# A re-planned order for a recurrence followed by a two-layer MLP: GpSimd idle from block 9, TensorE's instruction pages in the plan, and wider products of zeros

## The chip, the cores and the metric

The kernel runs on one core of one Trainium2 chip. The metric is the device time of one launch in microseconds, as the median of three runs. The engines of the core are TensorE (PE in the profile; PEld is its loading of weights), VectorE (DVE), ScalarE (ACT), GpSimd (POOL) and SyncE (SP), which issues nearly all DMAs. All of them run their own instructions in order and wait for each other by semaphores.

## What is computed

A gated linear recurrence over 768 steps for 4 batches of 8 heads with head dimension 48, and then a two-layer MLP on the 3072 tokens of 384 features that it gives:

```python
def _attn_ref(q, k, v, alpha):
    B, H, S, D = q.shape                       # 4, 8, 768, 48
    state = np.zeros((B, H, D, D))
    for t in range(S):
        state = alpha[:, :, t, :, None] * state + einsum('bhd,bhe->bhde', k[:, :, t], v[:, :, t])
        y[:, :, t] = einsum('bhd,bhde->bhe', q[:, :, t], state)
    return y

def _moe_ref(x, w_in, w_out, s, b):            # w_in 384 x 2048, w_out 2048 x 384
    r = np.maximum(x @ w_in, 0.0)
    return (s * (r * r) + b) @ w_out
```

Inputs and outputs are float32. There is no expert routing in this case: every token goes through both products.

## The kernel before

The tokens are cut into 24 blocks of 128 steps, six for each batch. In each block the recurrence is done in chunked form: products on TensorE in place of 128 single steps, and a state of one 48 x 48 matrix for each head that is handed from block to block. The MLP works on groups of two blocks (256 tokens).

The kernel has no loop over blocks that sets the order. One string, ORDER, lists some 960 tokens, and the last lines of the kernel walk through it and call one small function for each token. The token's name says what is done, its number for which block or piece, and a prefix (D:, A:, P:) which engine does it where that isn't the default engine of the name:

```python
    for t in ORDER.split():
        eng, name, i = token(t)
        FN[name](ENG[eng or DEF[name]], i)
```

So ORDER fixes the order on every engine, and tables beside it (C_BANK, A_BANK, H_BANK and so on) fix in which of the 8 PSUM banks each result stands, and R_BANK which of 4 buffers takes each relu. ORDER and the tables come from a planner outside of the kernel.

The tokens that matter here, with the block or piece as their number:

- a, k, q, v (and pa, pk, pq, pv for pairs of blocks): loads on SyncE (L172, L188). i and o: loads of the four pieces of w_in and w_out in float32 (L258, L261); ci and co cast them to bfloat16.
- ln, cum, eb, ei, el: logarithm of alpha on ACT, its running sum on TensorE, and the exponentials of it on ACT (L368, L373).
- qb, kb: q and k times those exponentials, on DVE or GpSimd (L234, as `qk`). T with Tc (first blocks) or Td (a transposing DMA on SyncE, L426): their transposes.
- A: the products of keys and queries in a block (L481; L491 for the first six); mk: the mask on them, on DVE (L502, L508). KV, t, sn: the state (L439, L466, and L234 as `s_st`). vc: the cast of v.
- y (for blocks 0 to 5 the parts ya and ys): the block's result from mask and state (L530, L544, L561); ye: its copy to SBUF as `xd`.
- m0 to m95: the first MLP product, eight tokens for each group of two blocks, six matmuls of 256 columns each (L592). re: relu out of PSUM, on ACT (L599) or DVE (L601). sq: the square, on ACT (L609) or DVE (L234 as `gt`).
- w0 to w95: the second MLP product, four tokens for each block, four matmuls of 384 columns each (L626; L618 for the last block). oe: scale and bias on DVE. st: the store.
- z0 and so on: products of zeros into a bank that nothing reads, between the early tokens (L659). The table FILLS says how many, of what width.

Products A, y, ya, ys and the early KV use parts of the array (64 rows, or 32 columns); m, w, T, cum and the later KV use all of it.

In the order before, GpSimd has 69 tokens: masks and zeroed tiles at the start, casts of weights, and over the whole run 16 of the 24 kb, 13 of the 24 qb, 11 of the 16 sn and 8 of the 24 vc.

Of the kernel before, what the change touches and what calls it, by code (L numbers as in the profile page):

```python
# [40 lines left out]
R_BANK = [3, 0, 2, 1, 2, 1, 0, 3, 2, 0, 3, 1, 1, 1, 1, 2, 2, 0, 3, 1, 0, 0, 1, 2, 3, 1, 1, 3, 1,
2, 0, 2, 0, 1, 3, 2, 2, 0, 2, 1, 1, 2, 0, 3, 3, 2, 0, 1, 0, 1, 3, 3, 1, 2, 0, 3, 2, 3, 3, 1, 3, 2,
1, 0, 1, 2, 2, 1, 3, 0, 0, 3, 2, 0, 3, 1, 1, 0, 1, 1, 2, 0, 2, 0, 1, 0, 2, 2, 0, 3, 1, 2, 3, 3, 1,
1]
FILLS = [(0, 32, 128), (1, 12, 128), (1, 4, 128), (1, 15, 128), (7, 12, 128), (7, 6, 128)]


ORDER = """
zz0 Us0 P:zqk0 P:zla0 pre0 pa0 Ui0 zt1 sml0 pk0 pa1 ln0 P:zla1 zs1 ln1 zqk2 zvp1 z0 cum0 eb0 ei0
pq0 cum1 pv0 ln2 el1 ln3 pq1 ei1 pk1 mp0 D:zt0 zqk1 zs0 id0 P:kb0 pa2 qb0 kb1 zvp5 D:zvp0 z1 cum2  # L50
el0 eb1 cum3 P:qb1 z2 T0 pv1 ei2 D:zvp2 Tc0 D:vc1 eb2 A:vc0 eb3 i0 z3 A0 P:qb3 i2 mk0 zvp4 el3 ei3
qb2 T1 KV1 pq2 pk2 KV0 P:kb3 zvp3 A:Tc1 el2 z4 A1 ya0 P:kb2 vc2 t0 mk1 t1 z5 T3 ys1 ya1 ln4 ln5 T2
cum5 i3 Tc3 A:vc3 ye1 KV3 KV2 ye0 Tc2 sn1 A3 cum4 eb5 A2 t2 el5 ei5 mk3 ci0 P:ci1 zs2 pv2 i1 ys2
el4 eb4 ei4 sn2 m0 m1 mk2 ys3 t3 P:ci5 re1 ya3 ya2 D:ci4 re0 sq0 qb5 ye3 ye2 m5 qb4 m4 m8 m9 P:ci7
o0 re5 re4 a6 A:sq4 A:sq5 kb5 sq1 re8 T5 kb4 m13 re13 T4 Tc5 ci6 A:sq13 m12 A5 D:re9 Tc4 D:of0 mk5
m7 sn3 m6 A:sq8 vc5 m15 s0 D:vc4 D:re12 A:sq9 o3 A4 re6 re7 ci2 KV5 KV4 m14 mk4 ci3 A:sq12 o1 o2
re15 m2 ya5 a8 a7 a9 k7 k6 A:sq15 ya4 ys4 t4 D:sn4 ys5 q6 D:co1 D:re14 P:co0 D:re2 D:ye4 v6 m10 m3
w0 w8 sm0 sq7 ln6 q7 v7 k8 sq6 A:sq14 re3 ye5 re10 U0 m21 m16 A:sq10 m11 re21 A:sq21 co7 sq2 sq3
ca0 se0 D:re16 P:co6 cum6 D:co3 el6 re11 A:sq11 ei6 ca3 sq16 m23 m18 w12 m17 m19 re18 ln8 D:re23
D:co2 re19 eb6 re17 ln7 ca1 D:co5 w4 D:co4 cb0 w9 m20 ca2 cb1 kb6 sq17 A:sq18 w13 A:sq19 cc0 qb6  # L60
cd0 D:re20 a11 a10 m22 cum8 w10 w1 cum7 w5 w11 w2 ei8 el8 eb7 ln9 el7 re22 qb7 w6 w14 bm0 w3 eb8
w7 ei7 A:sq22 be0 oe0 sq23 D:vc6 A:sq20 A:vc7 Td6 P:kb7 w20 w16 KV6 w15 w21 cum9 oe2 Td7 q8 t6
ln10 ei9 ln11 oe1 oe3 eb9 w22 A6 A7 w17 w18 w23 mk6 cum10 mk7 y6 y7 q9 KV7 oe5 D:ye7 k9 v9 v8 q10
k10 w19 eb10 ei10 ye6 el10 cum11 m31 el9 t7 oe4 P:qb8 m26 P:qb9 D:re31 kb8 A:vc8 ei11 m25 m24
D:re25 D:re24 m27 A:sq25 m29 eb11 A:sq24 P:kb9 D:re26 P:qb10 k11 Td9 D:re27 D:vc9 P:kb10 A:sq31
KV8 m30 w24 q11 Td8 w28 re30 KV9 A:sq26 a12 sq30 D:re29 sn7 t8 D:sn8 A:sq27 m28 w25 re28 A:sq28
A:sq29 A9 Td10 v10 A8 w29 t9 w26 ln12 mk9 v11 a13 w27 w30 mk8 cum12 y8 y9 A10 P:kb11 w31 P:qb11
ye8 oe6 sn9 D:vc10 el12 ye9 ln13 mk10 vc11 eb12 m37 KV10 Td11 m34 oe7 m36 t10 q13 k13 cum13 k12
a15 D:re34 A11 re36 re37 mk11 m35 ei12 el13 sq36 m39 eb13 m32 sn10 re39 ei13 a14 q12 q14 y11 v13
qb13 sq39 sq37 kb12 ye11 y10 P:kb13 D:re35 ln15 ye10 D:re32 A:sq35 m38 m33 m46 cum15 D:re33 A:sq32  # L70
m44 A:sq33 a17 D:re46 ln14 D:re38 sq38 m45 m42 w36 m41 cum14 Td13 A:sq46 sq34 el15 D:re42 D:re44
ln17 m40 A:sq44 P:qb12 Td12 k14 v12 w37 re45 el14 w38 w39 ei14 eb15 ei15 D:re40 A13 D:vc13 sq45
oe9 A12 A:sq40 mk12 v14 w32 mk13 m43 w33 re41 sq41 a18 a16 w34 A:vc12 eb14 re43 P:kb14 KV12 A:sq43
v15 m47 q15 sq42 t12 w35 A:vc14 ln16 y13 y12 qb14 ye12 w44 D:ye13 re47 cum17 v19 k15 cum16 oe8 k16
eb16 A:sq47 ei17 KV13 P:qb15 m53 v16 Td14 t13 w40 m48 kb15 D:re48 eb17 ln18 el16 re53 ei16 KV14
m55 w41 m52 D:re55 m50 Td15 A:sq55 re52 m54 P:kb16 vc15 w45 KV15 m51 D:sn13 A:sq48 re54 q17 D:re50
t14 D:vc19 A14 mk14 sn14 A:sq50 A15 mk15 t15 w42 w46 A:sq52 q18 A:sq54 w47 m49 y14 re51 y15 oe11
k19 k17 P:qb17 vc16 D:re49 D:sn15 KV16 w43 q16 ye14 ye15 m59 a19 A:sq49 ln19 A:sq51 sq53 qb16 k18
a20 a21 q20 P:kb17 cum18 m57 oe10 w52 m61 Td16 re57 D:re59 Td17 m56 w53 m58 q19 v17 A:sq57 ei18
sq59 D:re61 v18 cum19 ei19 el19 el18 eb18 w54 t16 m63 re58 A:sq61 w55 m62 D:re63 D:re56 sn16 eb19  # L80
P:kb18 sq58 P:kb19 q21 a22 A16 A17 mk17 oe13 ln20 w48 w49 cum20 k20 k23 vc17 w50 m60 w51 D:re62
ei20 el20 eb20 A:sq56 mk16 re60 P:qb19 y17 y16 w56 ln21 A:vc18 a23 ye17 ln22 qb18 KV18 cum21 ye16
ei21 P:kb20 t18 KV19 w57 cum22 A:sq63 Td18 eb21 ei22 k21 m67 ln23 eb22 oe12 sq60 P:qb20 Td19 t19
sq62 m71 w60 el21 P:qb21 D:re71 D:re67 m68 m69 el22 m66 w61 A:sq71 kb21 k22 v20 D:re68 re66 w62
P:kb22 A:sq67 A18 A19 A:sq66 D:re69 cum23 w58 w63 Td20 mk19 m64 Td21 q22 sn19 y19 mk18 y18 D:ye18
eb23 ye19 w59 m65 ei23 A:vc20 v22 oe15 oe14 sq69 m72 re65 A21 A20 m70 A:sq65 P:qb22 re64 re72 mk21
mk20 vc22 v21 A:sq64 m76 re70 vc21 m79 KV20 st2 q23 st0 P:kb23 A:sq68 A:sq70 st11 Td22 st8 st3
re79 w64 t20 qb23 sq79 w65 KV21 D:sn20 t21 w66 w67 w68 m77 re76 oe16 re77 A:sq76 w69 sq72 Td23 m74
# [22 lines left out]
def kernel(  # L111
# [15 lines left out]
    B, H, S, D = q.shape  # L127
# [201 lines left out]
    def o_cum(e, u):  # L329
        la = la_sb[u % NLA]  # L330
        ct_ps = BANK[C_BANK[u]]
        cum = ct_ps[:, 0:384].rearrange("a (r h d) -> a r h d", r=2, h=NP)
# [34 lines left out]
    def o_eb(e, u):  # L367
        e.activation(  # L368
            out=b_sb[u % NB].rearrange("a h d -> a (h d)"), in_=BANK[C_BANK[u]][:, 0:384], func=AF.Exp
        )  # L370

    def o_ei(e, u):
        e.activation(  # L373
            out=binv_sb[u % NB].rearrange("a h d -> a (h d)"), in_=BANK[C_BANK[u]][:, 0:384], func=AF.Exp,
            scale=-1.0,
        )

    def o_el(e, u):
        if u < NPB:
            n, g = u - u % 2, u % 2  # L380
            e.activation(
                out=blast_sb[:, n % NBL : n % NBL + 2, 2 * g : 2 * g + 2],
                in_=BANK[C_BANK[u]][:, 384:388].rearrange("a (p c) -> a c p", c=2), func=AF.Exp,
            )
        else:
            e.activation(out=blast_sb[:, u % NBL], in_=BANK[C_BANK[u]][:, 384:388], func=AF.Exp)

# [22 lines left out]
    def tview(u):  # L410
        return BANK[T_BANK[u]].bitcast(BF16)

# [18 lines left out]
    def kv_view(n):  # L431
        return BANK[KV_BANK[n]][:, 0:384].rearrange("a (p e) -> a p e", p=NP)

# [220 lines left out]
        e.dma_start(out=out[n * C : (n + 1) * C, :], in_=out_sb[n % NOS])  # L654

    def o_z(e, x):
        bank, m, w = FILLS[x]
        for _ in range(m):
            nc.tensor.matmul(  # L659
                out=BANK[bank][:, 0:w], lhsT=zeros[:, 0:128], rhs=zeros[:, 0:w], start=True, stop=True  # L660
            )


    def tri64(t, strict):
# [106 lines left out]
```

## Time and profile before

| what | before |
| --- | --- |
| median of 3 runs | 178.77 us (178.53 to 179.05) |
| the profiled execution | 179.38 us, of which the span from the first to the last instruction is 177.7 us |
| granted TensorE clock | 1.0 over the span |
| busy: TensorE, DVE, ACT, GpSimd | 169.5, 134.0, 111.3, 54.6 us |
| first MLP product, L592, 576 matmuls | 72.0 us |
| second MLP product, L626, 368 matmuls | 68.1 us |
| GpSimd, qk from k, L234, 16 instructions | 17.0 us, 1066 ns each |
| GpSimd, qk from q, L234, 13 instructions | 13.4 us, 1031 ns each |
| products of zeros, L659, 81 matmuls | 7.2 us |

Busy times of matmuls overlap their neighbours at both ends, so a mean of 273 ns for a 256-column matmul isn't the distance between two of them. A "wait" is idle time of an engine ahead of an instruction, put down to the instruction or the DMA that ended it; "issue" is idle time for which the profile shows no wait. The slices of the page cut the span into 40 parts of 4.44 us; a window such as 66:83 is in us from the start of the span.

### The profile page before, as it was taken

To read this page: it belongs to the slowest core of one execution; us is meant where nothing else is said; L and a number is where in the kernel's file an instruction comes from. 1 tells how busy PE (TensorE), PEld (TensorE's weight loads), DVE (VectorE), ACT (ScalarE), POOL (GpSimd) and SP (SyncE) were. 2 spreads that over 40 slices of the span, in tenths; PEclk is the share of its full clock that TensorE was granted. 3 is DMA by queue.
4 is the path that set the end of the run, shared out by engine and by line. 5 is a ranking of instruction groups with operands and counts; after the bars stand their busy time and mean duration, and the time that the engine had idled before them with its cause. 6 is when DMAs were issued, how large, how long until landed. Compare 5 with 4: busy or idle time off the path is not lost.

```text
span 177.7 us, 5545 instructions
## 1 busy us (share of the span) xinstructions
PE 169.5 (95%) x2289; PEld 127.7 (72%) x2289; DVE 134.0 (75%) x239; ACT 111.3 (63%) x242; POOL 54.6 (31%) x83
## 2 busy tenths in 40 slices
PE   7898799899999999999999999999999999999992
PEld 7787597677656786687767868767767688877672
DVE  2298889999977999999887789496978779634421
ACT  3867689798662467367686857559649544956000
POOL 7686512400023715214022352634235302000000
PEclk9999999999999999999999999999999999999999
DMA  5999999999799969999989999999979993000352
GB/s 146 325 318 289 271 329 360 313 280 199 141 224 191 200 144 198 146 203 174 192 171 226 128 209 184 197 210 186 207 127 266 185 344 139 4 0 0 141 208 98
DMA packets 113708, 34.96 MB, mean 197 GB/s; under 512 B 106900, under 2 KB 112148, under 8 KB 113684
## 3 DMA queue, kind: packets, MB, share of 16 engines
q1 hardware_dynamic: 113684, 34.61, 87.8%
q8 instruction: 18, 0.29, 0.7%
q14 instruction: 6, 0.05, 0.1%
HBM read 25.17 MB, written 4.72 MB: 168 GB/s over the span
## 4 chain that ended last, share of the span: by engine, by line
PE 71%; DVE 7%; SPq 7%; ACT 6%; DMA 4%; issue 3%; POOL 1%; DVEq 0%; ACTq 0%
PE bank_ps L626 31%; PE bank_ps L592 28%; SPq L188 5%; DMA wst<-in_moe_w_in_dram 4%; PE bank_ps L481 3%; ACT gt L609 2%; PE bank_ps L544 2%; DVE r L601 2%; ACT r L599 2%; PE bank_ps L335 2%; PE bank_ps L530 2%; SPq L258 2%; PE bank_ps L618 1%; DVE am L502 1%; PE bank_ps L439 1%
## 5 line engine op out<-in xcount | busy, mean ns | idle before, releaser
L592 PE MATMUL bank_ps<-xd,w_in_bf 128*128 128x256 bf16 x576 | 72.0, 273 | 1.8 <-DVE r L601 1.1
L626 PE MATMUL bank_ps<-w_out_bf,gt 128*128 128x384 bf16 x368 | 68.1, 326 | 0.0
L592 PEld LDWEIGHTS <-w_in_bf 128*128 128x128 bf16 x576 | 54.5, 98 | 12.2 <-issue 0.9
L626 PEld LDWEIGHTS <-gt 128*128 128x128 bf16 x368 | 34.5, 98 | 19.5 <-issue 0.2
L599 ACT ACTIVATE r<-bank_ps 128x512 bf16<-128x512 f32 x52 | 30.6, 597 | 16.6 <-PE bank_ps L592 11.9
L609 ACT ACTIVATE gt<-r 128x512 bf16<-128x512 bf16 x61 | 36.8, 628 | 5.4 <-DVE r L601 4.9
L601 DVE TENSOR_SCALAR r<-bank_ps 128x512 bf16<-128x512 f32 x44 | 29.3, 685 | 8.9 <-PE bank_ps L592 6.4
L234 POOL TENSOR_TENSOR qk<-k_in,binv 128x384 bf16<-128x384 f32 x16 | 17.0, 1066 | 39.3 <-ACT binv L373 26.6
L502 DVE TENSOR_TENSOR am<-bank_ps,U_bf 128x1024 bf16<-128x1024 f32 x18 | 21.5, 1220 | 4.1 <-PE bank_ps L481 3.6
L234 DVE TENSOR_TENSOR gt<-r 128x512 bf16<-128x512 bf16 x35 | 17.1, 507 | 3.5 <-ACT r L599 3.3
L641 DVE SCALAR_TENSOR_TENSOR wst<-bank_ps,s_col,bias_w 128x384 f32<-128x384 f32 x23 | 14.0, 614 | 6.9 <-PE bank_ps L626 6.4
L234 POOL TENSOR_TENSOR qk<-q_in,b_s 128x384 bf16<-128x384 f32 x13 | 13.4, 1031 | 17.4 <-DMA q_in<-in_q_dram 13.9
L373 ACT ACTIVATE binv<-bank_ps 128x384 f32<-128x384 f32 x24 | 11.9, 498 | 10.3 <-PE bank_ps L342 7.7
L234 POOL TENSOR_TENSOR s_st<-t,blast 128x384 bf16<-128x384 bf16 x11 | 9.4, 855 | 23.7 <-DVE t L466 23.6
L229 ACT ACTIVATE xd<-bank_ps 128x384 bf16<-128x384 f32 x19 | 9.4, 520 | 9.8 <-PE bank_ps L544 9.2
L324 ACT ACTIVATE la<-a_in 128x384 bf16<-128x384 f32 x24 | 12.3, 522 | 5.1 <-DMA a_in<-in_alpha_dram 5.1
L368 ACT ACTIVATE b_s<-bank_ps 128x384 f32<-128x384 f32 x24 | 12.0, 499 | 4.5 <-PE bank_ps L342 3.4
L466 DVE TENSOR_TENSOR t<-bank_ps,s_st 64x192 bf16<-64x192 f32 x32 | 11.3, 352 | 1.7 <-POOL s_st L234 0.6
L234 DVE TENSOR_TENSOR qk<-q_in,b_s 128x384 bf16<-128x384 f32 x11 | 6.0, 550 | 6.3 <-DMA q_in<-in_q_dram 5.9
L659 PE MATMUL bank_ps<-zeros 128*128 128x128 bf16 x81 | 7.2, 255 | 1.3 <-DVE half_bf L695 1.3
L508 DVE TENSOR_TENSOR am<-bank_ps,maskp 128x1024 bf16<-128x1024 f32 x6 | 7.3, 1223 | 0.7 <-PE bank_ps L491 0.6
L530 PE MATMUL bank_ps<-qkT,s_st 128*32 128x128 bf16 x240 | 6.8, 221 | 0.6 <-issue 0.6
(87 smaller groups left out, 156.9 us busy)
## 6 DMA issues: line engine op xcount, KB each, us to landing
out_dram<-wst SPq DMA_DIRECT2D x23, 192.0 KB, 3.1
a_in<-in_alpha_dram SPq DMA_DIRECT2D x18, 192.0 KB, 4.4
k_in<-in_k_dram SPq DMA_DIRECT2D x18, 192.0 KB, 3.9
q_in<-in_q_dram SPq DMA_DIRECT2D x18, 192.0 KB, 3.8
v_in<-in_v_dram SPq DMA_DIRECT2D x18, 192.0 KB, 3.8
wst<-in_moe_w_in_dram SPq DMA_DIRECT2D x4, 768.0 KB, 7.5
wst<-in_moe_w_out_dram SPq DMA_DIRECT2D x4, 768.0 KB, 7.6
a_in<-in_alpha_dram SPq DMA_DIRECT2D x3, 384.0 KB, 4.8
```

Source lines behind the costliest of these rows:

```text
L234: e.tensor_tensor(out=o, in0=x, in1=y, op=ALU.mult)
L324: e.activation(out=la_sb[u % NLA].rearrange("a (r h) d -> a r h d", r=2)[..., 0:D], in_=seen("a", u), func=AF.Ln,)
L368: e.activation(out=b_sb[u % NB].rearrange("a h d -> a (h d)"), in_=BANK[C_BANK[u]][:, 0:384], func=AF.Exp)
L373: e.activation(out=binv_sb[u % NB].rearrange("a h d -> a (h d)"), in_=BANK[C_BANK[u]][:, 0:384], func=AF.Exp, scale=-1.0,)
L466: e.tensor_tensor(out=t1_sb[n % 2][r, :, c], in0=kv[r, :, c], in1=s_sb[(n - 1) % 3][r, :, c], op=ALU.add,)
L502: e.tensor_tensor(out=am.rearrange("a e p t -> a (e p) t"), in0=a_ps.rearrange("a e p t -> a (e p) t"), in1=U_bf.unsqueeze(1).to_broadcast ...
L592: nc.tensor.matmul(out=hp[:, i * 256 : (i + 1) * 256], lhsT=w_in_bf[:, kk, 128 * j : 128 * (j + 1)], rhs=xd_sb[g % 3][:, kk, :], start=(kk ...
L599: e.activation(out=r_sb[R_BANK[w]], in_=BANK[H_BANK[w]], func=AF.Relu)
L601: e.tensor_scalar_max(r_sb[R_BANK[w]], BANK[H_BANK[w]], 0.0)
L609: e.activation(out=o, in_=r, func=AF.Square)
L626: nc.tensor.matmul(out=BANK[bank][:, 0:d_model], lhsT=gt_sb[:, j, c0 : c0 + C], rhs=w_out_bf[:, j, :], start=(j == 0), stop=(j == NJ - 1),)
L641: e.scalar_tensor_tensor(out=out_sb[n % NOS], in0=BANK[O_BANK[n]][:, 0:d_model], scalar=s_col[:, 0:1], in1=bias_w, op0=ALU.mult, op1=ALU.add,)
```

## The change

The order and all bank tables are new, and with them where each token runs. The number of tokens for each kind of work is the same, except that there are eight batches of zeros in place of six. The function o_z now takes a number of columns and cuts it into matmuls of up to 512 columns. No other function differs.

```diff
-FILLS = [(0, 32, 128), (1, 12, 128), (1, 4, 128), (1, 15, 128), (7, 12, 128), (7, 6, 128)]
+FILLS = [(0, 4288), (0, 1984), (0, 704), (0, 256), (6, 448), (0, 1856), (1, 448), (4, 256)]
...
     def o_z(e, x):
-        bank, m, w = FILLS[x]
-        for _ in range(m):
+        bank, cols = FILLS[x]
+        while cols:
+            w = min(cols, 512)
             nc.tensor.matmul(
                 out=BANK[bank][:, 0:w], lhsT=zeros[:, 0:128], rhs=zeros[:, 0:w], start=True, stop=True
             )
+            cols -= w
```

Of the order, the part around the first MLP products, and the part around the last GpSimd token of the order after (sn8):

```diff
-cum5 i3 Tc3 A:vc3 ye1 KV3 KV2 ye0 Tc2 sn1 A3 cum4 eb5 A2 t2 el5 ei5 mk3 ci0 P:ci1 zs2 pv2 i1 ys2
-el4 eb4 ei4 sn2 m0 m1 mk2 ys3 t3 P:ci5 re1 ya3 ya2 D:ci4 re0 sq0 qb5 ye3 ye2 m5 qb4 m4 m8 m9 P:ci7
+zvp5 pv2 D:sn1 kb3 P:ci0 i1 D:vc2 D:ye1 eb5 T2 Tc2 ei5 el5 eb4 ci1 T3 A:Tc3 D:zs2 KV3 KV2 t2 z6 A2
+m0 i3 mk2 a6 re0 m1 o0 a7 z7 ys2 A3 sn2 ya2 P:ci4 ys3 t3 mk3 a8 P:qb4 m4 ci5 ei4 qb5 m5 U0 ya3 kb4
...
-D:re25 D:re24 m27 A:sq25 m29 eb11 A:sq24 P:kb9 D:re26 P:qb10 k11 Td9 D:re27 D:vc9 P:kb10 A:sq31
-KV8 m30 w24 q11 Td8 w28 re30 KV9 A:sq26 a12 sq30 D:re29 sn7 t8 D:sn8 A:sq27 m28 w25 re28 A:sq28
+m27 cum11 m24 q11 D:re29 ln12 eb11 re24 KV8 ei11 w17 w18 D:re27 A8 t8 A9 mk8 m26 sn8 A:sq24 ei10
+mk9 w19 m31 y8 re26 y9 k10 A:sq29 a13 re31 oe4 A:sq31 ye9 ln13 k12 k14 v10 m30 cum12 q12 KV9 kb10
```

The tokens of each engine in the two orders, counted:

| tokens | before | after |
| --- | --- | --- |
| GpSimd in all | 69 | 42, the last one sn8 |
| kb on GpSimd, DVE | 16, 8 | 4, 20 |
| qb on GpSimd, DVE | 13, 11 | 6, 18 |
| sn on GpSimd, DVE | 11, 5 | 5, 11 |
| vc on GpSimd, DVE, ACT | 8, 8, 8 | 5, 7, 12 |
| re on DVE, ACT | 44, 52 | 38, 58 |
| sq on DVE, ACT | 35, 61 | 41, 55 |
| ye on DVE, ACT | 5, 19 | 9, 15 |
| casts of w_in on GpSimd, DVE, ACT | 3, 1, 4 | 6, 0, 2 |
| DVE in all, ACT in all, SyncE in all | 214, 240, 136 | 240, 241, 136 |
| products of zeros | 81 of 128 columns | 23 of up to 512, 10,240 columns |

The end of the order: before, `w91 w92 w93` are followed by `w94 w95`, and the stores st22, st23 and st24 are issued one after the other as their halves are ready. After, w94 and w95 stand ahead of `w91 w92 w93`, and the last three stores are issued as st22, st24, st23.

## The prediction

> **What bounds the kernel now.** I read the page's busy table first, then who made TensorE wait, then busy time by stretch, then single engines in time around each wait.
>
> ```profile
> PE 169.5 (95%) x2289; PEld 127.7 (72%) x2289; DVE 134.0 (75%) x239; ACT 111.3 (63%) x242; POOL 54.6 (31%) x83
> ```
>
> TensorE has 8.2 us without work in a span of 177.7. All waits of its matmuls (us in total, times, longest):
>
> ```profile
> PE bank_ps L659 <- DVE half_bf L695: 1.3, 1, 1.3
> PE bank_ps L592 <- DVE r L601: 1.1, 2, 0.7
> PE bank_ps L592 <- POOL w_in_bf L231: 0.6, 1, 0.6
> PE bank_ps L530 <- issue: 0.6, 1, 0.6
> ...
> PE bank_ps L544 <- DVE am L502: 0.4, 1, 0.4
> ```
>
> The first is the start. The timeline puts the third and fourth into the time in which w_in still comes in:
>
> ```profile
> 20.36 0.35 PE L530 MATMUL bank_ps<-qkT,s_st 128*32 128x128 bf16 x12 [0.57 <-issue]
> 20.64 0.81 PE L561 MATMUL bank_ps<-am,vp 64*32 64x128 bf16 x64
> 22.08 0.39 PE L592 MATMUL bank_ps<-xd,w_in_bf 128*128 128x256 bf16 x2 [0.62 <-POOL w_in_bf L231]
> ```
>
> So 22.08 is a gate: the second piece of w_in lands at 20.94 (the chain has its transfer last before that), GpSimd casts it, then the product goes. What TensorE does or loses before 22.08 is free up to 0.62. Behind the gate it is a conveyor: work in order, plus stalls. The stretches (TensorE, weight loads, DVE, ACT, POOL):
>
> ```profile
> 22.10:50.00 27.90, 27.16 (x342) 20.89 (x343) 26.24 (x47) 23.93 (x48) 4.65 (x9) 1.00 0.98 268
> 66.00:83.00 17.00, 16.18 (x254) 11.83 (x252) 15.92 (x27) 10.39 (x25) 6.48 (x7) 1.00 1.00 176
> 83.00:105.00 22.00, 22.00 (x250) 16.33 (x249) 17.35 (x32) 17.29 (x38) 6.25 (x7) 1.00 1.10 186
> 105.00:128.00 23.00, 23.00 (x308) 17.13 (x307) 18.52 (x34) 14.69 (x37) 8.31 (x10) 1.00 1.00 193
> 128.00:150.00 22.00, 22.00 (x302) 16.55 (x300) 17.75 (x30) 12.26 (x25) 5.78 (x8) 1.00 1.03 222
> ```
>
> Stalls behind the gate are 27.90 - 27.16 = 0.74 and 17.00 - 16.18 = 0.82, together 1.56; after 83 there is none. All three (at 34.40, 73.02, 82.39) wait for DVE. Just ahead of each, DVE has one instruction that ran while GpSimd ran one (timeline, three places, GpSimd's line first):
>
> ```profile
> 32.23 0.83 POOL L231 CAST w_out_bf<-wst 128x768 bf16<-128x768 f32 x1 [4.28 <-DMA wst<-in_moe_w_out_dram]
> 32.28 1.34 DVE L231 CAST w_out_bf<-wst 128x768 bf16<-128x768 f32 x1
> 66.64 1.00 POOL L234 TENSOR_TENSOR qk<-k_in,binv 128x384 bf16<-128x384 f32 x1 [3.58 <-ACT r L599]
> 66.67 1.25 DVE L234 TENSOR_TENSOR gt<-r 128x512 bf16<-128x512 bf16 x1
> 80.12 1.19 POOL L234 TENSOR_TENSOR qk<-k_in,binv 128x384 bf16<-128x384 f32 x1 [2.54 <-ACT binv L373]
> 80.37 1.36 DVE L234 TENSOR_TENSOR qk<-k_in,binv 128x384 bf16<-128x384 f32 x1
> ```
>
> The medians of the same DVE rows are 0.42 (gt) and 0.55 (qk); the w_out cast beside no GpSimd work takes 0.55. Each was stretched by about 0.8.
>
> **The change part by part.** The profiled execution took 179.38 us for a span of 177.7; the median of the runs is 178.77. I work in the span and put the difference on the median.
>
> Products of zeros: 81 of 128 columns (10,368) become 23 with 10,240 columns. A run of 12 takes 0.83, thus (0.83 - 0.255)/11 = 0.052 for 128 columns. A 512-column one is not in the trace; 256 columns go every 0.109 (36 in 4.09) and 384 every 0.163, so cost follows columns and I expect 0.21 to 0.22. All lie ahead of the gate: 0. The first batch grows from 4096 to 4288 columns, 0.17 more at its rate of 3.59 us for 4096, inside the 0.62.
>
> Pages: the 58 fewer products remove 116 TensorE instructions and move every boundary of 256. The page's instruction queue (q8) moved 18 packets with 0.29 MB, 16 KB each. The one stall of TensorE that no semaphore explains (0.57, between a weight load and its own product, while the DMA is over 90% busy) is what a late page looks like. It is hidden: the gate opens later anyway. I take 0; if the new order puts a late page behind the gate, it costs up to 0.57. The Trainium skill (Runtime: NRT & Kernel Launch, Instruction fetch mechanics) says that the sequencer fetches the next page ahead and that a crossing is mostly hidden; by it the planning of pages is worth 0 here. The trace disagrees for this one crossing, and the sum is the same by both.
>
> Work behind the gate: the new order keeps ya3 (32 small products) for after the first product of the second w_in piece. Two such tokens are the 64 in 0.81 above, so (0.81 - 0.22)/2 = 0.29 moves behind the gate. TensorE also changes the shape of its products (full array, 64 rows, 32 columns) 48 times behind the gate and not 46, counted in the two orders. The chain gives the price:
>
> ```profile
> 106.58 0.28 PE bank_ps L530 x12
> 106.86 0.22 PE bank_ps L544 x16
> 107.08 0.17 PE bank_ps L530 x12
> ```
>
> Entering costs 0.28 - 0.17 = 0.11, so 2 x 0.1 = 0.2. All else (96 + 96 MoE tokens, 20 A, 18 y, 17 KV) is the same. Sum +0.5.
>
> End: the last three stores are issued st22, st24, st23 with only w91 to w93 left, before one at a time. SyncE issues stores about 0.65 apart at the end, so the last comes 0 to 0.28 later; I take 0.1. Start of the gate: ci4 alone on GpSimd, with no cast on DVE beside it, may save up to 0.17 (1.08 against the mean 0.91); the order of the loads ahead of that piece carries the same bytes. I take 0.1 and the two cancel.
>
> GpSimd to DVE: from block 9, DVE gets 12 kb, 10 qb and 7 sn that were GpSimd's, 29 at about 0.55 = 16.0. In the whole order six re become ACT's (-6 x 0.685 = -4.1), six sq come to DVE (+6 x 0.42 = 2.5), four ye too (+4 x 0.56 = 2.2): +0.6. Gone is the stretching: 0.83 and 0.81 above, and between 105 and 165 the gt row's mean of 0.515 over its median 0.42, x16 = 1.5: together -3.1. ACT has 6 more re and 6 fewer sq (0.597 against 0.628) and four more vc; it is 63% busy: 0. SyncE has the same 136 steps, but a slot of q or k is now freed by DVE's queue, and the transpose stands behind those loads.
>
> What DVE's load is worth: neighbours on DVE overlap by about 0.08 (instructions that read a bank start 1.14 apart and last 1.22). Net load before: 22 to 50, (26.24 - 47 x 0.08)/27.9 = 81%; 66 to 83, (15.92 - 2.16)/17 = 81%; 83 to 105, 67%. After, over the 84 us from 66 to 150: recorded 69.5 + 16.0 + 0.6 - 3.1 = 83.0, less 152 x 0.08 = 12.2, is 70.8: 84%. Where DVE was 81% loaded TensorE lost 0.74 in 27.9 (2.7%); at 67% it lost nothing. So the 84 us cost between 0 (all of that loss was stretching) and 2.7% = 2.2. DVE waits in order, and behind each mask or kb that waits for TensorE or a load stand the re that free the banks for w_in products. I take the middle, 1.1: near the upper row in load, without its stretching.
>
> By the Trainium skill (SBUF — State Buffer, Who interferes with whom) DVE and GpSimd share one port pair under an exclusive lock, and the later one blocks wholly. The trace agrees (0.42 became 1.25 beside a GpSimd product of 1.00). By that rule alone both stalls after 66 vanish, which is the first rival.
>
> Sum: +0.5, stalls 0.74 (up to 66, GpSimd still works there) + 1.1 in place of 1.56, +0.3. Together +0.8: span 178.5, median 179.6.
>
> **The rivals.** (1) Faster: DVE keeps up at 84% since nothing stretches it. For: each stall follows a stretched instruction. Against: DVE is loaded from 66 to 150 without a slack stretch, so lateness is not made up. With the early stall 0.5 - 0.82 = -0.3 (178.45), with none 0.5 - 1.56 = -1.06 (177.7); a gate 0.2 earlier gives 177.5. (2) Slower by more: DVE is the bound from 66 to 150 at the full 2.7%: 0.5 + 0.74 + 2.2 - 1.56 = +1.9, 180.7; with a page behind the gate (0.57) and the end (0.28), 181.5. It decides where DVE idles more than the 16% left. (3) Nothing measurable: stalls merely move, with 0.5 to 1.6 of them: 178.2 to 179.3. (4) The change is not there, as GpSimd still runs in blocks 9 on: the order has no GpSimd step after sn8, so under 0.01.
>
> **How the numbers follow.** 0.3% is 0.54 us, about what a measurement of this kernel can tell from none. Forecast 0.30, (2) 0.16, both slower: 0.46. (1) beyond 0.3%: 0.36. (3) with the near part of (1): 0.18. Cases of both signs are close; the forecast's own range is 179.3 to 180.4. The range takes in (1)'s end and (2)'s with both extras: 177.5 to 181.5.
>
> **What would show it.** Right: the product of m4 starts at 21.9 to 22.2; no GpSimd work after about 70; DVE's gt and qk rows at 0.42 and 0.55 from then on; DVE over 80% net from 66 to 150, and TensorE's waits there name DVE r, am or t, 1 us or more in total. Wrong: no waits on DVE after 66 (rival 1); waits on the transposes or on ACT in their place, or a gate past 22.5 (early loads, pages), would be a cause I did not price.

## The result, and the profile after

The changed kernel took **183.16 us** (182.81 to 183.37, four runs) beside 178.65 for the kernel before: ratio 1.025, 95% interval 1.022 to 1.028. It is slower, by 4.5 us. The forecast was 179.6 with a range up to 181.5. The same kernel, run again later on two chips, gave 180.27 us (179.71 to 181.89, twelve runs; ratio 1.0093, 1.0059 to 1.0127) and 181.01 us (180.39 to 181.47, four runs; ratio 1.0124, 1.0074 to 1.0173). Medians here are of all runs of a kernel, while ratios and intervals leave out one run each of e2, e4, e6, e8 and e1_again that took over 1.5% more than the fastest of its kernel. So two things need a cause: the 1.4 to 2.4 us that the change always costs, and some 2 to 3 us that the first runs had on top.

The profiled execution after is one of 183.36 us with a span of 181.1. The page's busy times:

```profile
PE 170.1 (94%) x2230; PEld 123.1 (68%) x2231; DVE 142.2 (79%) x264; ACT 113.3 (63%) x243; POOL 30.8 (17%) x57
```

TensorE works as long as before (169.5) in a span 3.4 longer. (The spans differ by less than the 4.5 of the medians: the execution that was profiled before took 0.7 more than the median beside it and the one after 0.2 more, and the time outside of the span is 1.7 before and 2.3 after.) DVE has 8.2 us more work, not the 13.5 of the prediction's sum (16.0 + 0.6 - 3.1). The waits of TensorE's matmuls:

```profile
PE bank_ps L626 <- ACT gt L609: 1.6, 1, 1.6
PE bank_ps L303 <- DVE wst L287: 1.4, 1, 1.4
...
PE bank_ps L592 <- POOL w_in_bf L231: 1.0, 2, 0.6
```

Besides the tokens named above, co0 to co7 cast the halves of w_out's four pieces (o0 to o3; co6 and co7 those of o3), ca, cb, cc and cd add its rows up in place on DVE for the products bm0 and sm0 (bias and scale; se0 copies the latter's result), and s0 loads s and b. The two largest waits are new, and neither is a wait for the DVE load that the prediction priced. L626 is a product of the second MLP weight (w21) that waits for a square on ACT; L303 is the product bm0, which waits for DVE's column sums of w_out. The stretches (TensorE, weight loads, DVE, ACT, GpSimd, granted clock), the first line from the kernel before and the others from after:

```profile
50.00:66.00 16.00, 16.00 (x178) 11.28 (x177) 12.98 (x23) 7.17 (x18) 6.86 (x7) 1.00 1.03 192
22.10:50.00 27.90, 26.45 (x362) 19.87 (x361) 22.64 (x34) 20.40 (x42) 11.83 (x17) 1.00 0.97 250
50.00:66.00 16.00, 12.99 (x151) 8.45 (x150) 14.71 (x24) 8.59 (x21) 4.56 (x5) 1.00 0.99 190
66.00:83.00 17.00, 17.00 (x218) 12.79 (x215) 15.56 (x31) 13.20 (x29) 0.83 (x1) 1.00 0.95 187
83.00:105.00 22.00, 22.00 (x298) 16.45 (x296) 18.24 (x35) 16.88 (x37) 0.00 (x0) 1.00 1.12 188
105.00:128.00 23.00, 22.63 (x303) 16.52 (x301) 20.47 (x41) 16.41 (x40) 0.00 (x0) 1.00 1.04 185
```

Lost are 1.45 from 22 to 50 and 3.01 from 50 to 66, where the kernel before lost 0.74 and 0.00. From 66 on, where GpSimd is idle and where the prediction looked, only 0.37 is lost; from 128 to 150 nothing.

The sum by the distances between the starts of TensorE's products (everything over a product's usual distance by more than 0.15 counts as stall): the gate m4 starts 1.13 earlier (20.95 for 22.08), the stalls behind it are 6.06 in place of 1.98 (+4.08), the work between is +0.56, the tail behind the last matmul -0.08. That is +3.43, and the spans differ by 3.4. So nearly all of it is stalls, and 5.5 of the 6.1 lie ahead of 66. The two largest make 3.0 of them, and this is where they come from (timeline, four places):

```profile
47.98 0.84 ACT L229 ACTIVATE w_out_bf<-wst 128x768 bf16<-128x768 f32 x1 [2.81 <-DMA wst<-in_moe_w_out_dram]
50.61 0.96 DVE L287 TENSOR_TENSOR wst<-wst 128x768 f32<-128x768 f32 x1 [1.40 <-ACT w_out_bf L229]
51.99 1.80 PE L626 MATMUL bank_ps<-w_out_bf,gt 128*128 128x384 bf16 x10 [1.57 <-ACT gt L609]
55.55 0.91 PE L303 MATMUL bank_ps<-wst,ones_f 128*128 128x384 f32 x2 [1.44 <-DVE wst L287]
```

ACT stands 2.81 us for the last piece of w_out (o3). Its casts (co7, co6) are ahead of the square that w21 needs, since ACT works in order, and the column sums on DVE stand behind the casts. One late load, two waits. In the kernel before, SyncE had issued all four pieces by 32.5, and the last to come landed at 39.7. After, the issue of the third begins at 37.5 and that of the last at 40.2; the last lands at 47.96. SyncE's w_out issues, first before and then after:

```profile
27.46 5.04 SPq L261 DMA_DIRECT2D wst<-in_moe_w_out_dram  x3
```

```profile
30.17 2.42 SPq L261 DMA_DIRECT2D wst<-in_moe_w_out_dram  x1
37.51 0.40 SPq L261 DMA_DIRECT2D wst<-in_moe_w_out_dram  x1
40.19 3.41 SPq L261 DMA_DIRECT2D wst<-in_moe_w_out_dram  x1
```

The new order has k7, q7, v6 and s0 ahead of o1, and k6 and q6 ahead of o3. Some of these wait for GpSimd or DVE (k6 for 1.2 us, by the view of SyncE's waits, for a column sum on DVE), and all behind them on SyncE wait too.

### The profile page after: what moved, and what is told of

Read it like the earlier page. It is cut to its first block, busy times and chain, and to the rows that moved or that the text cites. A ratio compares the mean times of both kernels' runs of the same rounds, so it can differ in the third digit from the quotient of the medians.

```text
span 181.1 us, 5413 instructions
## 1 busy us (share of the span) xinstructions
PE 170.1 (94%) x2230; PEld 123.1 (68%) x2231; DVE 142.2 (79%) x264; ACT 113.3 (63%) x243; POOL 30.8 (17%) x57
## 4 chain that ended last, share of the span: by engine, by line
PE 64%; DMA 16%; SPq 8%; DVE 5%; issue 2%; ACT 2%; POOL 2%; DVEq 0%; POOLq 0%
PE bank_ps L626 26%; PE bank_ps L592 26%; SPq L188 5%; DMA q_in<-in_q_dram 5%; DMA wst<-in_moe_w_out_dram 4%; DMA a_in<-in_alpha_dram 4%; DVE wst L287 3%; DMA k_in<-in_k_dram 3%; PE bank_ps L481 2%; PE bank_ps L544 2%; PE bank_ps L530 2%; PE bank_ps L618 1%; PE bank_ps L439 1%; PE bank_ps L335 1%; SPq L172 1%
## 5 line engine op out<-in xcount | busy, mean ns | idle before, releaser
L626 PE MATMUL bank_ps<-w_out_bf,gt 128*128 128x384 bf16 x368 | 68.1, 326 | 1.7 <-ACT gt L609 1.6
L626 PEld LDWEIGHTS <-gt 128*128 128x128 bf16 x368 | 33.9, 98 | 21.7 <-ACT gt L609 2.0
L599 ACT ACTIVATE r<-bank_ps 128x512 bf16<-128x512 f32 x58 | 34.1, 597 | 16.8 <-PE bank_ps L592 12.3
L609 ACT ACTIVATE gt<-r 128x512 bf16<-128x512 bf16 x55 | 33.8, 628 | 6.5 <-DVE r L601 6.1
L601 DVE TENSOR_SCALAR r<-bank_ps 128x512 bf16<-128x512 f32 x38 | 25.4, 686 | 3.6 <-PE bank_ps L592 1.7
L234 DVE TENSOR_TENSOR qk<-k_in,binv 128x384 bf16<-128x384 f32 x20 | 10.9, 556 | 5.1 <-ACT binv L373 3.7
L229 ACT ACTIVATE xd<-bank_ps 128x384 bf16<-128x384 f32 x15 | 7.4, 510 | 6.1 <-PE bank_ps L544 5.5
L234 DVE TENSOR_TENSOR qk<-q_in,b_s 128x384 bf16<-128x384 f32 x18 | 9.9, 551 | 0.8 <-DMA q_in<-in_q_dram 0.5
L660 PE MATMUL bank_ps<-zeros 128*128 128x512 bf16 (+4 forms) x22 | 7.0, 436 | 1.4 <-DVE zeros L702 1.3
L234 POOL TENSOR_TENSOR qk<-q_in,b_s 128x384 bf16<-128x384 f32 x6 | 6.4, 1081 | 9.0 <-ACT r L599 5.6
L229 ACT ACTIVATE vp<-v_in 128x384 bf16<-128x384 f32 (+1 forms) x14 | 6.4, 470 | 1.8 <-DMA v_in<-in_v_dram 1.8
L231 DVE CAST xd<-bank_ps 128x384 bf16<-128x384 f32 x9 | 5.1, 564 | 2.8 <-ACT r L599 1.5
```

Source lines behind the costliest of these rows:

```text
L229: e.activation(out=o, in_=i, func=AF.Copy)
L234: e.tensor_tensor(out=o, in0=x, in1=y, op=ALU.mult)
L599: e.activation(out=r_sb[R_BANK[w]], in_=BANK[H_BANK[w]], func=AF.Relu)
L601: e.tensor_scalar_max(r_sb[R_BANK[w]], BANK[H_BANK[w]], 0.0)
L609: e.activation(out=o, in_=r, func=AF.Square)
L626: nc.tensor.matmul(out=BANK[bank][:, 0:d_model], lhsT=gt_sb[:, j, c0 : c0 + C], rhs=w_out_bf[:, j, :], start=(j == 0), stop=(j == NJ - 1),)
```

## The experiments

All have the order of the changed kernel as their base, save e4 and e5. Theory: the landing of o3 (read as the start of its first cast on ACT, where ACT stood waiting for it) sets the time. Rivals: ACT's head of line alone; DVE's load or GpSimd's idleness; pages. I give edits of the order as the tokens that move.

**Loads or ACT's order (one chip, before 178.94).**

e1, both late pieces loaded as soon as GpSimd's cast of the piece in the same buffer stands ahead in the order:

```diff
- ... ys5 ya4 A:sq12 mk5 o1 ya5 k6 re2 q6 m10 D:ye4 re8 ye5 ln7 ln6 m15 o3 re10 ...
+ ... KV4 P:ci2 o1 A:sq13 re9 ... D:re12 P:ci6 o3 of0 m8 ...   (o1 and o3 gone from their old places)
```

> The order after, with one thing moved: SyncE issues the w_out pieces o1 and o3 right behind the steps that free their slots (ci2, ci6), ahead of s0, k6, q6. Theory L (late weights): after lost its time because o3 was issued at 40.19 and landed at 47.96; ACT stood in order before co7 so that sq19 and then w21 came late (wait 1.6), and DVE's column sums of w_out came late so that the bias product waited (1.4). Then o3 lands several us earlier, both waits shrink to under 0.5 each, and the time falls by 2 to 3.5 us from 183.2 to 180 to 181. Rival G (GpSimd idle, the prediction's own reason): the loss is DVE's and ACT's extra load, and moving two loads changes less than 0.5 us.

Measured 179.96 us (ratio 1.0051, 1.0024 to 1.0077), span 177.6. Both waits are gone; the longest left is 0.8 at the state product sm0 (0.98 in the expectation of e1s, which goes by the distance from the product before).

e2, ACT's two casts of that piece behind the square that w21 needs, loads untouched (one half of the piece is cast here after the column sum has been added into it, which changes that part of the weights):

```diff
- ... re19 co7 a9 k8 A:sq14 el8 ei8 co6 cb0 ca3 ... cd0 A:sq19 re23 ...
+ ... re19 a9 k8 A:sq14 el8 ei8 cb0 ca3 ... cd0 A:sq19 co7 co6 re23 ...
```

> The order after, with only ACT's two casts of the last w_out piece (co7, co6) moved behind sq19; the loads stay. Theory L in its narrow form (ACT's queue alone is what the late piece holds up): the wait of w21 on sq19 (1.6) goes and the time falls by 2 us or more. Theory L in its wide form (the column sums are held up as well): w21's wait goes, but the bias product meets the same late sums with TensorE earlier, its wait grows from 1.4 to about 2.5 to 3, and the time falls by 0 to 1 us. Rival G: no change.

Measured 180.23 (1.0053, 1.0025 to 1.0081). w21's wait is gone, and bm0's fell to 0.6: one column sum no longer stood behind a cast, and o3 landed at 46.7, 1.2 earlier than in the first runs.

e1b, e1 with k7, q7 and v6 behind o3 as well:

> As e1_loads, and k7, q7, v6 also stand behind o3, so that nothing but a6, a7, a8 comes between the w_out pieces. Theory L: the last piece lands some 2 us earlier still, but the bias product's wait is nearly gone already; k7, q7 and v6 come later by the time of two pieces (about 5 us), and kb7 on GpSimd started at 38.9 with its A7 only at 53.7. So within 0.7 us of e1_loads. Rival G: within 0.5 us of after.

Measured 183.01 (1.0211, 1.0157 to 1.0266). This missed: q7 comes late, its product with the exponentials (qb7) waits on DVE, the relu re22 stands behind that, and the running sum cum8 behind the relu. TensorE's first wait:

```profile
PE bank_ps L335 <- DVE r L601: 2.8, 1, 2.8
```

bm0's wait of 1.4 came back too, though the last piece had landed at 40.5: its casts stood behind that relu on ACT. So these three loads can't be the ones that come late either.

e4, the kernel before with the first part of the change alone: its kb, qb and sn from block 9 on go to DVE and its vc to ACT, at their old places.

> The order before, with one part of the change alone: from block 9 on the kb, qb and sn of GpSimd go to DVE and its vc to ACT, all at the same places of the order. The prediction's reason (DVE at 84% from 66 to 150 loses TensorE 1.1, up to 2.2 us, less the 0.8 of stalls behind stretched instructions): 0.3 to 1.5 us slower than before. Theory L, by which GpSimd's part cost nothing in after (no wait on DVE above 0.4 us after 66): between 0.8 us faster (both stalls behind stretched instructions gone) and 0.3 us slower than before.

Measured 186.77 us (1.0446, 1.0404 to 1.0488): 7.8 us slower, and both sides missed it. From 66 to 150 TensorE was busy 79.47 of 84 us. The profiled run, the fastest of the five, has a span 5.1 over the kernel before. Its longest waits past 66 name a transpose (1.2 at 70.5), ACT (0.7 at 83.7, 0.5 at 95.2) and DVE's relu (0.6 at 133.8). An idle GpSimd is dear in this order, which isn't planned for it; which of these queues is the first cause isn't shown.

**What e1 and e2 left open (one chip, before 178.94).** I first read e1 and e2 as gains of 3 us over 183.16. These four go on from there.

e1s, e1 with sm0 and se0 moved behind w13:

> The order of e1 (w_out's second and fourth piece loaded as early as their buffers allow) with one thing more: the state product sm0 and its exponent se0 stand four steps later on TensorE, behind the MoE product w13. In e1 sm0 was the longest wait left (0.8 for DVE's r, 0.98 by the distance of its start from the one before). If a wait at one place is simply lost time for the conveyor, 0.8 to 1.0 goes: 179.0 to 179.2, ratio to the kernel before about 1.000, and no wait of over 0.5 behind the gate. Rival: what sm0 waited for is late for others too (the DVE queue is full between 47 and 55, 91% busy), so the next step that needs DVE inherits the wait: 179.8 to 180.0 as in e1, with a new wait of 0.5 to 1 between 50 and 56.

Measured 179.83 (1.0043, 1.0010 to 1.0077). sm0's wait is gone, and a wait of 1.0 for a transpose came at 64.8. The time is the rival's; its place (50 to 56) and its cause (DVE) aren't.

e2b, e2 without its change of the weights: co7, co6 and behind them ca3, cb1, cc0 and cd0 stand after sq19.

> The changed kernel with only ScalarE's queue changed, loads where they were: its two casts of the last w_out piece (co7, co6) stand behind the activation sq19 that w21 waits for, and the column sums that read that piece (ca3, cb1, cc0, cd0) still behind those casts. In e2 one of the sums had come ahead of its cast and so both waits of the changed kernel (1.57 at w21, 1.44 at bm0) went at once. Theory: two separate victims of one late load. Here w21's 1.57 goes, since sq19 no longer stands behind the load, and bm0's 1.44 stays or grows a little, since the sums still follow the load: 181.4 to 182.0. Rival: the waits are one chain in which the time saved at w21 is waited for again at bm0, whose sums end at 55.5 whatever stands ahead: bm0's wait grows to about 3.0 and the time stays at 182.8 to 183.3.

Measured 179.73 (1.0061, 1.0027 to 1.0095). The waits are as the theory has them (none at w21, 1.62 at bm0), yet the time is 1.7 lower than it said. The reason was in the trace: the piece had landed earlier, with nothing changed ahead of it on SyncE's queue. Its first cast starts at 46.44, not 47.98, and ACT came to it from other work without a wait; the landing itself is at 45.81. So the 6.62 that the expectation of e10 takes from here as the distance from the landing to bm0 is the distance from the cast, and from the landing it is 7.25.

e7, e1 with the 29 kb, qb and sn of block 9 and later back on GpSimd:

> The order of e1 with the first part of the change undone: the 29 steps kb, qb and sn of block 9 and later that GpSimd had before the change go back to GpSimd, at their places. e1 is the comparison (179.96; from 66 to 150 it lost 0.6 of TensorE's time). Theory: a DVE at 84% keeps up as long as nothing stretches it, so leaving GpSimd idle is worth little by itself in this order; with GpSimd back, DVE has 16 us less work and some instructions stretched by 0.8 each, so stalls of about 0.8 come back at one to three places: 180.0 to 182.0, TensorE's new waits behind stretched DVE instructions or behind GpSimd itself. Rival (the one in which idle GpSimd was a cost here): DVE has air again and the 0.6 lost after 66 goes: 179.2 to 179.5.

Measured 180.49 (1.0078, 1.0048 to 1.0109), TensorE busy 83.86 of the 84 us from 66 to 150; its one long wait (1.4 at sm0, for the small load of s and b) lies ahead of that. Against e1 the difference is inside the intervals. In the new order, with its relus on ACT, GpSimd can work or idle from block 9 on: neither costs anything that these runs show.

e6, the changed kernel with zeros of 128 columns:

> The changed kernel with products of zeros of 128 columns again, the same columns in all (81 products in place of 23 or so): 116 TensorE instructions more ahead of the gate, so every boundary of 256 instructions lies elsewhere than planned. By the prediction's terms both the products and the pages are worth nothing: within 0.4 of the changed kernel (182.8 to 183.6), the waits of 1.6 (w21) and 1.4 (bm0) unchanged. Rival: pages matter where they were planned; a late page stands behind the gate at one or two places as a wait of 0.5 to 0.6 that no engine releases: 183.7 to 184.4. A second rival: narrow products start the clock or the early chain otherwise and the gate moves by over 0.3.

Measured 181.76 (179.74 to 185.6; ratio 1.0101, 1.0012 to 1.019). Two waits appear for which no semaphore is the cause:

```profile
PE bank_ps L491 <- issue: 1.1, 1, 1.1
PE bank_ps L561 <- issue: 0.9, 1, 0.9
```

They end at TensorE's 705th and 1217th instruction (a product and the weight load behind it go on together, so it is the 704th or the 705th as one counts). 705 = 193 + 2 x 256 and 1217 = 193 + 4 x 256; the stall of 0.57 in the kernel before also ended at its 705th, and e4 stood 1.15 at the same place. The first of the two lies on the path: m4 started at 22.07, and in the changed kernel at 20.95. But w21's wait was gone here too, and again o3 had landed early (46.7). That asked for a control.

**The control, and the zeros (one chip, before 178.86).** The changed kernel again, with nothing altered:

> The changed kernel once more, unchanged, as the control that the experiments on it need: e2b (loads where they were, ScalarE's casts moved) and e6 (only the products of zeros narrow) both lost the 1.57 wait at w21, and in both the last w_out piece also landed 1.2 to 1.5 us earlier (46.4 and 46.7, not 47.96) with the same queue. If the 183.2 belong to the kernel: 182.8 to 183.4 again, o3 landing at about 48 and both waits there. Rival: the landing of o3 is a matter of the run, the waits come only where it lands after 47, and the kernel gives 180 to 181.5 in some runs: then part of what e2b and e6 seemed to gain is not theirs.

Measured 180.27 us over twelve runs: the rival. Its profiled run has a span of 178.2, o3 lands at 45.35, and the wait at w21 has shrunk with it:

```profile
45.35 0.84 ACT L229 ACTIVATE w_out_bf<-wst 128x768 bf16<-128x768 f32 x1 [1.49 <-DMA wst<-in_moe_w_out_dram]
49.36 1.80 PE L626 MATMUL bank_ps<-w_out_bf,gt 128*128 128x384 bf16 x10 [0.24 <-ACT gt L609]
52.93 0.91 PE L303 MATMUL bank_ps<-wst,ones_f 128*128 128x384 f32 x2 [1.44 <-DVE wst L287]
```

With it my reading of e1, e2, e1s and e2b as gains of 3 us falls: against this control they gain 0 to 0.5 by the medians, 0.6 to 0.9 by the ratios to the kernel before, and the intervals overlap.

e8, e1 with zeros of 128 columns:

> The order of e1 (loads early, so no late w_out piece) with products of zeros of 128 columns: the same columns, 116 TensorE instructions more ahead of the gate. In e6 TensorE stood still twice for nothing that a semaphore shows, 1.12 at its 705th instruction and 0.88 at its 1217th, in the kernel before 0.57 at its 705th: 705 - 193 = 2 x 256, 1217 - 193 = 4 x 256. If these are late pages of 256 instructions, they come here at the same two products (705th and 1217th), 0.6 to 1.2 each, and both lie on the path, since TensorE and not a load sets the pace from 18.3 on: 181.2 to 182.4, against 179.96 of e1. Rival, by which pages are worth nothing: what is lost early is absorbed by the loads behind it: 179.7 to 180.3.

Measured 180.88 (179.85 to 182.63; 1.0111, 1.0077 to 1.0146), between the two. The profiled run has no wait at either product, but others. So of two profiled runs with narrow zeros one has these stalls and one hasn't; what they cost on average these runs don't settle.

e5, the kernel before with wide zeros and its own order:

```diff
-FILLS = [(0, 32, 128), (1, 12, 128), (1, 4, 128), (1, 15, 128), (7, 12, 128), (7, 6, 128)]
+FILLS = [(0, 4096), (1, 1536), (1, 512), (1, 1920), (7, 1536), (7, 768)]
```

> The kernel before with the products of zeros of 512 columns alone, order untouched: 116 TensorE instructions fewer, so each boundary of 256 falls on a product some 116 instructions later in the order than before. By the prediction's terms: the products themselves 0 (all ahead of the gate), so within 0.4 of the kernel before (178.5 to 179.4); the 0.57 at the 705th instruction goes or moves. Rival: without a plan for the pages a boundary falls on a busy stretch behind the gate and costs 0.6 to 1.1 there: 179.5 to 180.1.

Measured 178.77 (0.9990, 0.9966 to 1.0014): the zeros are worth nothing, as priced. Its profiled run stood 1.17 at the 705th instruction, ahead of the gate, and lost nothing by it.

**The dose (one chip, before 178.66).** Is the landing the cause, or does it go along with something else?

> The changed kernel a third time, as the middle dose for the three kernels beside it. In two profiled runs of it, its column product bm0 began 7.58 us (after_again: 45.35 to 52.93) and 7.59 us (47.96 to 55.55) behind the landing of the last w_out piece, o3; without waits it would have begun at 51.25 (52.93 less its 1.44 and w21's 0.24). So I expect, wherever o3 lands here, bm0 at that time + 7.6 and a span of 178.2 + (landing - 45.35): 180 to 181 us if it lands at 45 to 46, 183 if at 48. Rival: the 2.9 us were something else of that session, and span and landing don't go together.

Measured 181.01: o3 at 47.14, waits of 0.76 and 1.44, span 179.7 (the law of the expectation says 180.0):

```profile
47.14 0.84 ACT L229 ACTIVATE w_out_bf<-wst 128x768 bf16<-128x768 f32 x1 [2.03 <-DMA wst<-in_moe_w_out_dram]
51.15 1.80 PE L626 MATMUL bank_ps<-w_out_bf,gt 128*128 128x384 bf16 x10 [0.76 <-ACT gt L609]
```

e9, o3 later by intent:

```diff
- ... ln7 ln6 m15 o3 re10 A:sq10 ... q9 ... a10 m14 ...
+ ... ln7 ln6 m15 re10 A:sq10 ... q9 ... a10 o3 m14 ...
```

> The changed kernel with the load of the last w_out piece (o3) moved two loads later on SyncE's queue, behind q9 and a10. It should be issued about 41 and land at 47.5 to 48.5, as in the first runs of the changed kernel. Theory (landing sets the time): bm0 at landing + 7.6, waits of 1 to 2 at w21 and 1.4 at bm0, span 180.5 to 181.5, 182.3 to 183.5 us; 2 to 3 over the changed kernel beside it. Rival (the landing only goes along with it): within 0.5 of the changed kernel beside it.

Measured 183.29 us (182.72 to 183.69; 1.0243, 1.0184 to 1.0302), beside 181.01 for the kernel without that edit, and the intervals don't overlap. One load moved by two places costs 2.3 us, so the landing is a cause and doesn't only go along:

```profile
48.97 0.84 ACT L229 ACTIVATE w_out_bf<-wst 128x768 bf16<-128x768 f32 x1 [4.57 <-DMA wst<-in_moe_w_out_dram]
52.98 2.96 PE L626 MATMUL bank_ps<-w_out_bf,gt 128*128 128x384 bf16 x10 [3.30 <-ACT gt L609]
56.41 1.11 PE L303 MATMUL bank_ps<-wst,ones_f 128*128 128x384 f32 x2
```

The waits came otherwise than expected, 3.30 at w21 and none at bm0: behind w21 the granted clock was half (last section), so TensorE reached bm0 no earlier than its sums.

Six profiled runs in one table, e1's first two and then those of the changed order with a landing behind 45:

| kernel | o3 lands | bm0 starts | between | span |
| --- | --- | --- | --- | --- |
| e1 | 43.74 | 51.63, no wait | 7.89 | 177.6 |
| e1_again | 44.51 | 52.17, no wait | 7.66 | 177.8 |
| after_again | 45.35 | 52.93 | 7.58 | 178.2 |
| after_third | 47.14 | 54.72 | 7.58 | 179.7 |
| after, first | 47.98 | 55.55 | 7.57 | 181.1 |
| e9 | 48.97 | 56.41 | 7.44 | 181.9 |

In the last four w21 begins 4.01 behind the landing (49.36, 51.15, 51.99, 52.98). From the first of them to the last the landing moves by 3.6 and the span by 3.7, so from about 45 on a microsecond of landing is about a microsecond of the kernel; single steps go from 0.8 to 1.7. (e6 fits it: 46.7, bm0 at 53.7, span 179.4. e1_third isn't in the table, since a late small load and a half clock hold TensorE up ahead of bm0 there: 44.2, 54.3, span 179.4.) The waits at w21 and bm0 grow by only 1.3 of the 2.9 between after_again and the first runs. The rest are stalls ahead of w21 (at 27.4, 34.9, 41.2 and 44.7), which shorten its wait and don't move it.

e10, e9 with ACT's casts and the sums behind sq19 as in e2b:

> e9 with ScalarE's casts co7 and co6 moved behind sq19 and the four sums behind them (as in e2b). In e2b bm0 began 6.62 behind the landing, not 7.58, so the theory gives a span 0.7 to 1.0 shorter than e9's for the same landing, all of what is left of the wait at bm0 and none at w21: 181.3 to 182.6 us. Rival: ScalarE's head of line is what makes a late piece dear, so that with it gone a landing of 48 costs no more than one of 46: 179.7 to 180.4, as e2b.

Measured 184.53 (182.53 to 184.88; 1.03, 1.0228 to 1.0372). bm0 starts 6.48 behind the landing (49.68). So of the 7.6 the order on ACT makes 1.1, as the theory says, and the piece stays dear without it. The time is over both: here the granted clock halved behind bm0's single wait of 3.71 (last section), and the part behind the start of bm0 took 127.0 us, against 125.0 to 125.5 in the last four of the table.

> e1 again beside the changed kernel on the same chip: o1 behind ci2 and o3 behind ci6, landing at about 43.7, which is just ahead of the 43.7 (51.25 - 7.58) from which the theory lets a landing cost anything. So no wait at w21 or bm0, whatever the session: 179.5 to 180.2, 0.3 to 0.8 under the changed kernel if that lands at 45 to 46. Rival: another wait of the same size comes in its place (in the first run 0.98 at sm0): equal to the changed kernel within 0.2.

Measured 180.32 (1.0096, 1.0058 to 1.0134), 0.7 under the changed kernel on the same chip, with no wait at w21 or bm0 and 0.9 at sm0. The intervals overlap, so the gain is likely and not shown. No version of the new order beat the kernel before; the nearest is e1s at 1.0043.

**DVE's load (one chip, before 178.51).** e11, e1 with nine re given back to DVE, as the order before had them:

```diff
- re32 re34 re46 re49 re59 re62 re68 re71 re75          (on ACT)
+ D:re32 D:re34 D:re46 D:re49 D:re59 D:re62 D:re68 D:re71 D:re75
```

> The order of e1 with nine re between 66 and 150 us (re32, 34, 46, 49, 59, 62, 68, 71, 75, all of which the order before had on DVE) put back from ScalarE to DVE at their places: DVE gets 9 x 0.685 = 6.2 us, ScalarE loses 9 x 0.6 = 5.4. Net load of DVE there: (61.2 + 9 x 0.605) / 84 = 79%, against 73% in the changed kernel. Theory (the load of DVE costs TensorE from about 75 to 80% on, as the prediction's row of 2.7% at 81% has it): 0.5 to 1.8 us over e1 beside it, TensorE's new waits between 66 and 150 named DVE r, am or t. Rival (the load doesn't matter as long as nothing stretches DVE's instructions): within 0.4 of e1.

> e1 once more as the comparison for e11_dve_re on the same chip: 179.6 to 180.4, no wait at w21 or bm0, 0.1 to 0.6 of TensorE's time lost between 66 and 150.

e11 took 185.59 us (1.0375, 1.0321 to 1.0429), e1_third 180.68 (1.0117, 1.0078 to 1.0156): 4.9 us for 6.2 us of DVE work that ACT had room for. The theory had the sign and the kind of wait, at little over a third of the size. The profiled runs, both with a half clock from 45 to 48, differ by 4.8 in the span. e1_third lost nothing from 66 to 150; e11 lost 3.75, and its stretch there ends in

```profile
128.00:150.00 22.00, 19.90 (x272) 14.63 (x271) 17.81 (x35) 13.27 (x28) 0.00 (x0) 1.00 0.89 195
```

with a wait of 1.99 for DVE's mask. e1_third itself missed its bound of 180.4. In its profiled run (181.34, the longest of the four) the small load of s and b came late, 1.45 at sm0, and the clock halved behind that.

## Why the prediction was wrong, step by step

**The step that failed: "SyncE has the same 136 steps".** I counted the loads and did not follow their order. Of a step that is moved its place in the queue counts: o1 and o3 moved behind k7, q7, v6, s0, k6 and q6, and the last w_out piece lands at 45.4 to 48.0. For it I had priced 0 and kept "stalls 0.74 (up to 66)". Measured are 5.53 of stall up to 66 in the first runs (6.06 less 0.53 later on) and 2.71 in after_again (3.00 less 0.29). The two waits on the late piece are 3.0 of the 5.5 and 1.7 of the 2.7. The rest are shorter waits, in the first runs for a cast of w_in at 27.4 and for ACT's exponentials at 41.2. The last sentence of the prediction named the class, waits on ACT and early loads as "a cause I did not price", and that is what came.

**The gate.** I took 0.1 earlier, arguing that the loads ahead of the second w_in piece carry the same bytes. m4 started 1.13 earlier: the piece's load was issued at 11.54 and not at 12.90, its cast on GpSimd begins at 19.46 and not at 20.94, and TensorE, not the load, now sets the pace from the first product (18.07 to 20.95; 2.9 in after_again and after_third too). A term mis-sized by 1.0, this time in favour of the change; it hides as much of the stalls.

**Work behind the gate, +0.5.** Measured +0.56 (+0.65 in after_again). Right.

**The end, +0.1.** Measured -0.08 from the last matmul to the span's end. Nothing, as good as right.

**Zeros 0 and pages 0.** Right in the sum: e5 at 0.999, and no page stall behind the gate after. That a late page always hides is too strong: the kernels not planned for them stood 0.57, 1.15, 1.17, 1.12 and 0.88 at instructions 193 beyond a multiple of 256, and in e6 the 1.12 moved m4; the planned one lost 0.2 at most to "issue" in three profiles. That these places are page boundaries is inferred from the spacing alone, and no run here shows that the planning gains time. The rule that I quoted, that a crossing is mostly hidden (Trainium skill, Runtime: NRT & Kernel Launch, Instruction fetch mechanics), agrees with the traces as far as its "mostly" goes: TensorE runs some 4,500 instructions, about 17 times 256, and stood at one or two of these places or at none.

**DVE from 66 to 150, 1.1 (0 to 2.2).** Measured 0.37, and 0.12 in after_again. The load I worked out, 84%, did not come: reckoned the same way it is (72.6 - 139 x 0.08) / 84 = 73%. I had used the "six re" of the whole order. In the stretch itself nine left DVE, and of the 29 tokens of GpSimd 25 came into it; the groups of DVE from 66 to 150, first before and then after:

```profile
L601 DVE TENSOR_SCALAR r<-bank_ps 128x512 bf16<-128x512 f32 x27 | 18.0, 685 | 6.0 <-PE bank_ps L592 5.2 <-ACT r L599 0.4 <-ACT gt L609 0.2
L234 DVE TENSOR_TENSOR gt<-r 128x512 bf16<-128x512 bf16 x19 | 9.4, 510 | 0.2
```

```profile
L601 DVE TENSOR_SCALAR r<-bank_ps 128x512 bf16<-128x512 f32 x18 | 12.2, 687 | 1.1 <-ACT gt L609 0.4 <-PE bank_ps L592 0.4
L234 DVE TENSOR_TENSOR gt<-r 128x512 bf16<-128x512 bf16 x22 | 8.9, 418 | 0.3 <-ACT r L599 0.2
```

e11 puts these nine back and loses 4.9 us. So the danger that the forecast and rival (2) saw is real, much larger than 2.7%, and the new order avoids it with ACT's help. e4 never moved them and loses 7.8, but no run moves them alone in its order, so that they are the reason there isn't shown.

The reckoning of the load was wrong as well. The busy time of a view counts an overlap once already (from 22 to 50 before, the 47 instructions add up to 29.1 us and the view has 26.24), so taking 0.08 off for each instruction counted the overlap twice. Where the kernel before lost time DVE was busy 94% and not 81%, and from 83 to 105, where it lost nothing, 79% and not 67%. Nor is the share a price. From 66 to 150 DVE was busy 83% of the time before, 86% after, 88% in e4 and 88.5% in e11, and TensorE lost 0.82, 0.37, 4.53 and 3.75 us there. So it must matter where in DVE's order the work stands; that is argued from these four and not tested.

**The rivals.** Rival (1)'s mechanism held where it was meant to: no stretched DVE instructions after 66 (gt 418 ns on average where it was 510), and the 0.82 lost from 66 to 83 is gone. It came out slower all the same, in part for the loads. Rival (2) had a size near the first result and the wrong cause. Rival (4), as said, was not there.

**What stays open.** Why the same queue lets the piece land at 45.35 in one run and at 47.98 in another: both loads in the chain ahead of it took longer (the load of alpha 6.70 and 7.57 us, o3 itself 6.93 and 7.77), and nothing in the kernel says why. And of the 1.4 to 2.4 us that the change always costs, e1 takes away at most 0.7; the 1.0 to 2.2 us of e1 over the kernel before are work (+0.5), sm0 and small waits that I did not take apart. Some of it is e1's own: its order puts s0 behind o3, and sm0 waits for that small load in e1_third (1.45), e7 (1.4) and e8 (0.8). The profiles can't place the rest, for e1's span of 177.6 is no longer than the 177.7 of the execution profiled before, which was one of the longer ones of its kernel.

## What to carry to other kernels

When an order is re-planned, follow every queue through it, the one that only issues DMAs first: find the last load that each wait depends on, and compare its place in the queue and not only the count of the loads. Run the changed kernel again as a control beside the experiments; without it, four kernels here would have been credited with 3 us that belonged to the occasion. And count moved work inside the stretch in which it matters, since totals over the whole kernel can hide a planner's trade.

## What the runs showed of the hardware

TensorE's granted clock halved behind the longest waits here, and this can make a long wait dearer than its length: in e10 the part behind bm0 took some 1.5 us more for it. In e9, with 3.30 us of wait up to 52.98, the clock is half from 53.5 to 56.5:

```profile
53.50:54.00 0.50, 0.50 (x3) 0.30 (x2) 0.50 (x1) 0.50 (x3) 0.12 (x1) 0.50 0.74 124
56.50:57.00 0.50, 0.50 (x1) 0.41 (x2) 0.50 (x2) 0.00 (x0) 0.00 (x0) 0.65 1.05 210
```

The Trainium skill (TensorE: Matmul & The Clock Gate, Part 1) gives half rate after an idle window of about 3.4 us, until a busy one has passed. The time at half rate agrees, and so do e9 and e10 (3.71). The threshold does not always: in e1_third the clock was half from 45 to 48 behind a wait of only 1.45 (TensorE was busy 1.3 of the 3 us from 41 to 44), and in the changed kernel two waits of 1.57 and 1.44 left it at 1.00. What decides between these two isn't shown.

SyncE's issue of a load can itself take about as long as a small load takes to land (3.8 to 4.4 us for 192 KB on the page of the kernel before): 3.41 us for the last w_out piece, and 3.52 for a load of v at 15.60, without a wait that the profile shows, while earlier loads were under way. (Of the 4.12 for the first w_out piece it puts 3.4 down to a wait for GpSimd.) All that stands behind it on the queue waits that long.
